# A fused retention and two-layer kernel on one core: the order of operand rounding, product sums and weight rounding in the second layer

## The chip, the cores and the metric

The kernel runs on one NeuronCore of a Trainium2 chip. Its time is the device time of one execution in microseconds (us); less is better. One execution was profiled as well, and all rows of a trace come from that one.

## What is computed

Attention with decays (retention) over 4 batches, 8 heads, 576 positions and 64 values a head gives a matrix x of 2304 x 512. Two layers follow, each of two matrix products with a nonlinearity between them:

```python
ret = (q @ k.T / 8) * Dmat            # per head; Dmat[i, j] = gamma ** (i - j) for i >= j, else 0
x = (ret @ v) as 2304 x 512
h = x @ w_in;  x = maximum(0.01 * h, h) @ w_out          # first layer, 512 -> 2048 -> 512
h = x @ w2_in; y = where(h > 0, h, exp(minimum(h, 0)) - 1) @ w2_out   # second layer
```

All inputs are float32. The kernel keeps float32 accuracy with a faster matmul type (`F32R`): each operand is split in a rounded high part and the low rest, and a product of two numbers takes three matmuls (high x high, high x low, low x high).

## The kernel before, in words

**Tiling.** The 2304 rows are four blocks of 512 and a small one of 256 (`SIZES`). The 2048 middle columns are four quarters `q` of four tiles of 128. Each layer runs quarter by quarter, in it block by block. The results of a quarter stand in PSUM ("y" banks, four) and are added into `yp` in SBUF at the end of each block (`evac`, line 576 on DVE, line 574 on ACT in the first quarter).

**Order.** Everything stands under a manual schedule: each engine runs its instructions in the order of the program text, and an instruction that waits holds all behind it on its engine. Five queues matter: TensorE (PE), VectorE (DVE), ScalarE (ACT), GpSimd (POOL), and SyncE (SP), which issues the DMAs. Generators cut long chains into steps: `go(steps, n)` runs n steps, `spot(n)` runs n steps of the waiting second matrix products (`pending`), `side()` runs one step of a stage. So the text interleaves TensorE's work with that of the other engines.

**First layer.** A loop over 72 units (`units`, line 584; a unit is one tile of one block, in the small block two tiles). A unit does `moe_h` (product 1, then `gh` and `g` on ACT and `gl` on DVE), and `moe_y` of the unit three before (`LAG`). Beside it the weights are split: `split_a` (two ACT passes from the raw weight), `split_b` (four DVE passes, in steps `split_ops`), `split_c` (ACT rounds the high part, POOL or DVE subtracts the low part).

**Second layer.** Its first matrix product is done with seven products of half-size operands in place of eight (`seventh`, numbers 0 to 6; in the trace 12 matmuls of 256 columns each). It needs sums of operands and sums of results:
- operand sums, `stage(blk)`: from the first layer's `yp` it makes differences `t1` to `t4` (`less`, DVE, line 642), rounds seven tiles (`put`: ACT line 636, then POOL or DVE line 638), and sends them to DRAM in four transfers (`send`, line 648). They come back as `xo` (`load_x`, line 680). The stages of blocks 0, 1 and 2 start at units 60, 64 and 68, that of block 3 behind the loop. The tiles `xs` and `xo` and the weight sums `ws` share one pool of eight slots (`xpool`, tag "x").
- weight sums: `sums_a` (four POOL additions, lines 693 to 696), `sums_b` (ACT rounds, line 705; POOL subtracts, line 706).
- result sums, in `seven`: `copy_of` copies a product from PSUM (ACT, line 844: p1, p5, p53), `add_up` adds (DVE, line 839: c11, c12, c22). Product 3 overwrites the bank of p5, so it waits for that copy; products 5 and 6 go on in the bank that c12 and c22 read, so they wait for these sums. c21 stays in the bank.

Each result then goes through `elu`: two ACT passes (lines 738, 740), one DVE pass (742), an ACT rounding (746) and a DVE subtraction (748) into `gg`, from which `second_y` does the second matrix product in four steps of 12 matmuls (6 in the small block, `small_y`).

A block of `seven` thus runs on TensorE: products 0, 1, 2; a step of `second_y` of the block before; products 3, 4; a step; product 5; a step; product 6; a step. In the first block of a later quarter these steps are the small block's, half as long. In the very first block they are the first layer's last three units. Two weights of a coming use are split in each block (`rounds`), and on DVE these passes stand between the sums:

```python
        p53 = copy_of(z)
        seventh(a, q, blk, 4)
        c12 = add_up(a, p53)
        if r[1]:
            go(rest)
```

Of the kernel before, what the change touches and what calls it, by code (L numbers as in the profile page):

```python
# [10 lines left out]
F32 = mybir.dt.float32  # L11
# [80 lines left out]
def retention_moe(  # L92
# [531 lines left out]
    def stage(blk):  # L624
# [6 lines left out]
        def room(k, ops=2):  # L631
            kept[k] = xpool.tile([P, ops, 2, 2, n], F32R, tag="x", name="xs")

        def put(k, i, x):
            hi, lo = kept[k][:, i, 0], kept[k][:, i, 1]
            nc.scalar.activation(hi, x, AF.Copy)  # L636
            by = nc.gpsimd if i == 0 else nc.vector
            by.tensor_tensor(lo, x, hi.bitcast(F32), ALU.subtract)
# [12 lines left out]
        room(0)  # L651
        put(0, 0, b11)
        put(0, 1, b21)
        yield
        send(0)
        t1 = less(b12, b11)
        room(1)
        put(1, 0, t1)
        put(1, 1, b22)
        yield  # L660
        send(1)
        t2 = less(b22, t1)
        t3 = less(b22, b12)
        room(2)
        put(2, 0, t2)
        put(2, 1, t3)
        yield
        send(2)
        t4 = less(b21, t2)
        room(3, 1)  # L670
        put(3, 0, t4)
# [63 lines left out]
    def elu(c, out, cut):  # L735
# [6 lines left out]
        nc.vector.scalar_tensor_tensor(t, t, -1.0, c, ALU.add, ALU.max)  # L742
        t = t.rearrange("p (s n) -> p s n", s=2)
        hi, lo = out[:, 0, :, cut], out[:, 1, :, cut]
        yield
# [47 lines left out]
    def small_h(q, gg):  # L793

        n = SMALL
        for f in range(FQ):
# [18 lines left out]
            if f % 2:  # L815
                g = bpool.tile([P, DM], F32, tag="t", name="g", bufs=3)
# [38 lines left out]
    def seven(q, blk, room, rounds, keep, side):  # L855
# [4 lines left out]
        r = list(rounds) + [None] * (2 - len(rounds))  # L860

# [7 lines left out]
        seventh(a, q, blk, 0, True)  # L869
        if r[0]:  # L870
            split_a(r[0])
        p1 = copy_of(a)
        if r[0]:
            split_b(r[0])
            load_next()
# [6 lines left out]
        p5 = copy_of(z)  # L882
        spot()
        side()
        g1 = room()
        e11 = elu(c11, g1, slice(0, n))
        go(e11, 3)
        if r[0] and not keep and blk:
            split_c(r[0])
        go(e11)  # L890
        seventh(z, q, blk, 3)
        fetch(2)
        if r[1]:
            split_a(r[1])
            rest = split_ops(r[1])
            go(rest, 3)
# [3 lines left out]
        if r[1]:  # L900
            go(rest)
            load_next()
        e12 = elu(c12, g1, slice(n, 2 * n))
        go(e12, 2)
        spot()
        side()
        for key in r[:1] * (blk == 0) + r[1:] * (blk > 0):
            if key and not keep:
                split_c(key)
# [281 lines left out]
```

## Time and profile before

| | us |
|---|---|
| median of 3 runs | 856.83 (856.0 to 857.05) |
| the profiled execution | 856.92 |
| its span on the core | 855.1 |
| TensorE busy | 814.6 (95%) |
| DVE, ACT, POOL busy | 531.3, 443.5, 176.4 |
| mean granted clock of TensorE | 0.978 |

The span is what the trace covers; 1.8 us lie around it. Granted clock 1.00 is 2.4 GHz, 0.50 is 1.2 GHz. TensorE is the busy engine throughout, so the idle stretches ahead of its matmuls, and the stretches at the lower clock, are where time can lie. The page shows the span in 40 slices of 21.4 us, each digit the busy share in tenths:

```profile
PE   9899999999999999998896889989999899989998
...
PEclk9999999999999999999897989999999999999999
```

The second layer's first block begins at 444.30; its quarters follow from 561, 656 and 751.

### The profile page before, as it was taken

The numbers are of one execution on the slowest core, as the hardware profiler recorded it, in microseconds if no ns is written. First come the engines' busy times: TensorE is split into PE (matmuls) and PEld (weight loads), VectorE is DVE, ScalarE is ACT, GpSimd is POOL, SyncE is SP. The second block draws the span as 40 slices with busy tenths as digits, with TensorE's granted clock in tenths as the row PEclk, the third lists the DMA queues.
The fourth block names the chain that finished last, engine by engine and source line by source line (L and its number), as shares of the span: only waits on it lengthen the run. The fifth ranks groups of instructions, "written<-read, shape, count | busy, mean of one in ns | idle before, by whom it ended". The sixth has DMA issues, their size and how long they took to land.

```text
span 855.1 us, 13359 instructions
## 1 busy us (share of the span) xinstructions
PE 814.6 (95%) x5240; PEld 723.1 (85%) x5240; DVE 531.3 (62%) x861; ACT 443.5 (52%) x755; POOL 176.4 (21%) x160
## 2 busy tenths in 40 slices
PE   9899999999999999998896889989999899989998
PEld 6778888888888888887796779779989799879997
DVE  6998943465266625566677756556775677665453
ACT  3456445662244524454545666667665666554442
POOL 2565521000000000015351323221222113210000
PEclk9999999999999999999897989999999999999999
DMA  9995320121011200026488677446570675525612
GB/s 337 330 307 172 132 87 26 50 74 50 1 50 50 74 25 29 22 74 221 172 295 281 235 252 272 189 172 242 203 268 4 258 253 210 191 89 185 242 51 74
DMA packets 34670, 133.64 MB, mean 156 GB/s; under 512 B 4144, under 2 KB 7472, under 8 KB 26928
## 3 DMA queue, kind: packets, MB, share of 16 engines
q1 hardware_dynamic: 34320, 132.66, 43.5%
q8 instruction: 41, 0.67, 0.3%
q14 instruction: 21, 0.17, 0.1%
q10 hardware_dynamic: 288, 0.14, 0.1%
HBM read 113.38 MB, written 19.40 MB: 155 GB/s over the span
## 4 chain that ended last, share of the span: by engine, by line
PE 35%; DVE 7%; ACT 6%; issue 4%; DVEq 0%; ACTq 0%
PE ps_y L406 18%; PE ps_h L406 17%; DVE c L839 2%; ACT gg L746 1%; DVE t L742 1%; ACT t L738 1%; ACT t L740 1%; DVE raw L367 1%; DVE u L372 1%; DVE u L369 1%; DVE yp L576 1%; ACT yp L574 1%; DVE gg L748 1%; ACT xs L636 0%; ACT u L355 0%
## 5 line engine op out<-in xcount | busy, mean ns | idle before, releaser
L406 PE MATMUL ps_y<-woh,gg 128*128 128x512 f32 x580 | 185.5, 382 | 0.2 <-ACT yp L574 0.2
L436 DVE TENSOR_TENSOR gl<-g,gh 128x512 fp32r<-128x512 f32 x64 | 45.7, 714 | 136.6 <-ACT g L430 136.2
L406 PEld LDWEIGHTS ps_y<-woh,gg 128*128 128x128 f32 x580 | 111.1, 192 | 14.8 <-ACT yp L574 0.7
L406 PE MATMUL ps_h<-xo,ws 128*128 128x256 f32 x768 | 102.4, 290 | 21.4 <-DVE c L839 18.4
L406 PEld LDWEIGHTS ps_h<-xo,ws 128*128 128x128 f32 x768 | 98.5, 205 | 26.4 <-DVE c L839 21.5
L429 ACT ACTIVATE gh<-ps_h 128x512 fp32r<-128x512 f32 x64 | 38.2, 597 | 153.6 <-PE ps_h L406 153.5
L406 PE MATMUL ps_y<-gh,woh 128*128 128x512 f32 x288 | 112.1, 389 | 5.8 <-DVE yp L576 5.6
L406 PE MATMUL ps_y<-gl,woh 128*128 128x512 f32 x288 | 110.5, 384 | 0.0
L406 PE MATMUL ps_y<-wol,gg 128*128 128x512 f32 x290 | 110.3, 380 | 0.0
L406 PE MATMUL ps_y<-gh,wol 128*128 128x512 f32 (+1 forms) x288 | 106.7, 371 | 0.7 <-POOL wol L387 0.7
L406 PE MATMUL ps_h<-xh,wih 128*128 128x512 f32 x256 | 97.7, 382 | 1.0 <-ACT wih L385 0.8
L406 PE MATMUL ps_h<-xh,wil 128*128 128x512 f32 x256 | 97.6, 381 | 0.9 <-POOL wil L387 0.9
L387 POOL TENSOR_TENSOR wol<-u,woh 128x512 fp32r<-128x512 f32 x20 | 26.4, 1322 | 333.0 <-ACT woh L385 333.0
L406 PE MATMUL ps_h<-xo,wih 128*128 128x256 f32 x384 | 70.1, 276 | 4.2 <-DVE c L839 4.2
L748 DVE TENSOR_TENSOR gg<-t,gg 128x512 fp32r<-128x512 f32 x64 | 55.0, 862 | 26.2 <-ACT gg L746 25.1
L406 PEld LDWEIGHTS ps_y<-gh,woh 128*128 128x128 f32 x288 | 55.3, 192 | 14.9 <-issue 6.0
L406 PE MATMUL ps_h<-xl,wih 128*128 128x512 f32 x256 | 66.6, 383 | 0.0
L406 PEld LDWEIGHTS ps_h<-xo,wih 128*128 128x128 f32 x384 | 60.9, 192 | 6.6 <-DVE c L839 5.8
L742 DVE SCALAR_TENSOR_TENSOR t<-t,c 128x512 f32<-128x512 f32 x48 | 37.4, 778 | 45.1 <-ACT t L740 45.1
L406 PEld LDWEIGHTS ps_y<-gh,wol 128*128 128x128 f32 x288 | 55.3, 192 | 8.3 <-POOL wol L387 1.1
L406 PEld LDWEIGHTS ps_y<-gl,woh 128*128 128x128 f32 x288 | 55.2, 192 | 7.4
L406 PEld LDWEIGHTS ps_y<-wol,gg 128*128 128x128 f32 x290 | 55.9, 193 | 5.8
(113 smaller groups left out, 1478.8 us busy)
## 6 DMA issues: line engine op xcount, KB each, us to landing
xo<-x SPq DMA_DIRECT2D x48, 1024.0 KB, 6.4
raw<-in_moe_in SPq DMA_DIRECT2D x32, 512.0 KB, 3.8
raw<-in_moe_out SPq DMA_DIRECT2D x32, 512.0 KB, 3.7
x<-xs SPq DMA_DIRECT2D x12, 1024.0 KB, 6.3
ain<-in_att SPq DMA_DIRECT2D x16, 512.0 KB, 6.9
xo<-x SPq DMA_DIRECT2D x16, 512.0 KB, 4.9
ain<-in_att SPq DMA_DIRECT2D x20, 256.0 KB, 7.4
out<-yp SPq DMA_DIRECT2D x17, 256.0 KB, 2.3
```

What stands on the lines that cost most here:

```text
L367: nc.vector.tensor_scalar(high, high, 0x80000000, None, ALU.bitwise_and)
L369: nc.vector.tensor_scalar(u, u, W_LEAST, W_MOST, ALU.max, ALU.min)
L372: nc.vector.scalar_tensor_tensor(x, x, 3, high, ALU.logical_shift_left, ALU.bitwise_or)
L387: engine.tensor_tensor(l, u, h.bitcast(F32), ALU.subtract)
L406: nc.tensor.matmul(out, w, x, **flags)
L429: nc.scalar.activation(gh, h, AF.Prelu, alpha=0.01)
L436: nc.vector.tensor_tensor(gl, g, gh.bitcast(F32), ALU.subtract)
L574: nc.scalar.activation(t, y[e], AF.Copy)
L576: nc.vector.tensor_tensor(t, t, y[e], ALU.add)
L742: nc.vector.scalar_tensor_tensor(t, t, -1.0, c, ALU.add, ALU.max)
L748: nc.vector.tensor_tensor(lo, t, hi.bitcast(F32), ALU.subtract)
L839: nc.vector.tensor_tensor(t, x, y, ALU.add)
```

## The change

Nothing is computed in another way; the same instructions are issued in another order, from partly other buffers.

- `stage` goes in nine steps in place of five: a step rounds on ACT (`high`), the next subtracts (`low`) and takes the differences for the next pair. In the first layer's loop `side()` is called twice a unit, and behind the loop until no stage is left, so that the stages of blocks 0 to 2 end ahead of `seven`. The last block's stage starts one call later (`late`) and takes two of its four tiles from the pool `big`. `seven` calls `side()` four times in place of three.
- `sums_b` of the first weight pair moves to the unit after `sums_a`; that of later pairs moves from the end of block 2 into block 3, behind the rounding of e11.
- In `seven`: p1 is copied ahead of `split_a`; c11 and e11's two ACT passes stand ahead of `split_b`; e11's last subtraction stands behind c12; the second weight's `split_a` stands behind e11's DVE pass, its `split_b` behind c12 (in the first block of a quarter behind c22) with the last pass behind c22; e12's last subtraction stands behind c22.
- `small_h` has a step more, so that `spot` (matmuls and `evac`) stands ahead of its `elu` passes.

```diff
@@ -629,13 +629,15 @@
         kept = {}
 
         def room(k, ops=2):
-            kept[k] = xpool.tile([P, ops, 2, 2, n], F32R, tag="x", name="xs")
-
-        def put(k, i, x):
-            hi, lo = kept[k][:, i, 0], kept[k][:, i, 1]
-            nc.scalar.activation(hi, x, AF.Copy)
+            where = (big, "big") if blk == NMAIN - 1 and k % 2 == 0 else (xpool, "x")
+            kept[k] = where[0].tile([P, ops, 2, 2, n], F32R, tag=where[1], name="xs")
+
+        def high(k, i, x):
+            nc.scalar.activation(kept[k][:, i, 0], x, AF.Copy)
+
+        def low(k, i, x):
             by = nc.gpsimd if i == 0 else nc.vector
-            by.tensor_tensor(lo, x, hi.bitcast(F32), ALU.subtract)
+            by.tensor_tensor(kept[k][:, i, 1], x, kept[k][:, i, 0].bitcast(F32), ALU.subtract)
...
-        room(0)
-        put(0, 0, b11)
-        put(0, 1, b21)
+        def pair(k, *xs):
+            room(k, len(xs))
+            for i, x in enumerate(xs):
+                high(k, i, x)
+            yield
+            for i, x in enumerate(xs):
+                low(k, i, x)
+
+        yield from pair(0, b11, b21)
+        t1 = less(b12, b11)
         yield
         send(0)
-        t1 = less(b12, b11)
-        room(1)
-        put(1, 0, t1)
-        put(1, 1, b22)
+        yield from pair(1, t1, b22)
+        t2 = less(b22, t1)
+        t3 = less(b22, b12)
         yield
         send(1)
-        t2 = less(b22, t1)
-        t3 = less(b22, b12)
-        room(2)
-        put(2, 0, t2)
-        put(2, 1, t3)
+        yield from pair(2, t2, t3)
+        t4 = less(b21, t2)
         yield
         send(2)
-        t4 = less(b21, t2)
-        room(3, 1)
-        put(3, 0, t4)
+        yield from pair(3, t4)
         yield
         send(3)
-    def elu(c, out, cut):
+    def elu(c, g, j, cut):
...
         nc.vector.scalar_tensor_tensor(t, t, -1.0, c, ALU.add, ALU.max)
+        yield
         t = t.rearrange("p (s n) -> p s n", s=2)
-        hi, lo = out[:, 0, :, cut], out[:, 1, :, cut]
-        yield
+        hi, lo = g[j][:, 0, :, cut], g[j][:, 1, :, cut]
         nc.scalar.activation(hi, t, AF.Copy)
         yield
         nc.vector.tensor_tensor(lo, t, hi.bitcast(F32), ALU.subtract)
@@ -813,6 +816,7 @@
             nc.scalar.activation(t, h[:, n:], AF.Copy)
             nc.vector.tensor_tensor(t, t, h[:, :n], ALU.add)
             if f % 2:
+                yield
                 g = bpool.tile([P, DM], F32, tag="t", name="g", bufs=3)
...
-    def seven(q, blk, room, rounds, keep, side):
+    def seven(q, blk, room, rounds, keep, side, begun=None):
...
+        head = blk == 0
+        g = []
...
@@ -867,12 +874,9 @@
         fetch(0)
         a = bank("h", 4)
         seventh(a, q, blk, 0, True)
+        p1 = copy_of(a)
         if r[0]:
             split_a(r[0])
-        p1 = copy_of(a)
-        if r[0]:
-            split_b(r[0])
-            load_next()
         b = bank("h", 4)
         seventh(b, q, blk, 1, True)
         fetch(1)
@@ -880,53 +884,65 @@
         z = bank("h", 4)
         seventh(z, q, blk, 2, True)
         p5 = copy_of(z)
+        e11 = elu(c11, g, 0, slice(0, n))
+        go(e11, 2)
+        if r[0]:
+            split_b(r[0])
+            load_next()
         spot()
         side()
-        g1 = room()
-        e11 = elu(c11, g1, slice(0, n))
-        go(e11, 3)
-        if r[0] and not keep and blk:
-            split_c(r[0])
-        go(e11)
+        g.append(room())
+        go(e11, 1)
+        if r[1]:
+            split_a(r[1])
+        go(e11, 1)
+        if begun:
+            sums_b(begun)
         seventh(z, q, blk, 3)
         fetch(2)
-        if r[1]:
-            split_a(r[1])
-            rest = split_ops(r[1])
-            go(rest, 3)
         p53 = copy_of(z)
         seventh(a, q, blk, 4)
         c12 = add_up(a, p53)
-        if r[1]:
-            go(rest)
-            load_next()
-        e12 = elu(c12, g1, slice(n, 2 * n))
+        go(e11)
+        if r[0] and not keep and not head:
+            split_c(r[0])
+        e12 = elu(c12, g, 0, slice(n, 2 * n))
         go(e12, 2)
+        rest = split_ops(r[1]) if r[1] else iter(())
+        if not head:
+            go(rest, 3)
+            go(e12, 1)
         spot()
         side()
-        for key in r[:1] * (blk == 0) + r[1:] * (blk > 0):
-            if key and not keep:
-                split_c(key)
-        go(e12)
+        if r[0] and head:
+            split_c(r[0])
+        if not head:
+            go(e12, 1)
         seventh(a, q, blk, 5)
         fetch(3)
         c22 = add_up(a, p5)
-        g2 = room()
-        e22 = elu(c22, g2, slice(n, 2 * n))
+        go(e12, 1 + head)
+        e22 = elu(c22, g, 1, slice(n, 2 * n))
         go(e22, 2)
-        spot(2 if blk == 0 and q > 0 else 1)
-        if r[1] and not keep and blk == 0:
+        go(rest)
+        if r[1]:
+            load_next()
+        go(e12)
+        spot(2 if head and q > 0 else 1)
+        if r[1] and not keep:
             split_c(r[1])
         side()
+        g.append(room())
         go(e22, 1)
         seventh(a, q, blk, 6)
-        e21 = elu(a, g2, slice(0, n))
+        e21 = elu(a, g, 1, slice(0, n))
         go(e21, 2)
         go(e22, 1)
         go(e21, 1)
         over.extend((e22, e21))
-        pending.append(second_y(q, blk, (g1, g2)))
+        pending.append(second_y(q, blk, g))
         spot()
+        side()
@@ -1000,6 +1016,16 @@
                 split_a(begun[-1])
 
         stages = deque()
+
+        def side():
+
+            if stages and next(stages[0], end) is end:
+                stages.popleft()
+
+        def late():
+            yield
+            yield from stage(NMAIN - 1)
+
@@ -1022,9 +1048,12 @@
             moe_h(u)
             for key in rounded:
                 split_c(key)
+            if sums and not weights.get(("s", FT)) and n < 66:
+                sums_b(("i", FT))
+                weights["s", FT] = True
             if rounded == [("i", FT + 1)]:
                 sums_a(("i", FT))
-                sums_b(("i", FT))
+            side()
...
@@ -1052,8 +1081,7 @@
                 moe_y(p)
             if n in (60, 64, 68):
                 stages.append(stage((n - 60) // FQ))
-            if stages and next(stages[0], end) is end:
-                stages.popleft()
+            side()
@@ -1082,18 +1110,15 @@
...
-        def side():
-            if stages and next(stages[0], end) is end:
-                stages.popleft()
-
-        side()
-        stages.append(stage(NMAIN - 1))
+        while stages:
+            side()
+        stages.append(late())
         for q in range(NQ):
             for blk in range(NB):
                 if blk < NMAIN:
                     rounds = [splits.pop(0) for _ in range(min(2, len(splits)))]
                     held = rounds if blk == NMAIN - 1 else []
-                    seven(q, blk, room if (q, blk) != (0, 0) else big_room, rounds, bool(held), side)
+                    seven(q, blk, room if (q, blk) != (0, 0) else big_room, rounds, bool(held), side, begun if held else None)
...
@@ -1101,24 +1126,24 @@
                         )
                     if rounds and blk >= 2:
                         sums_a(rounds[0])
-                        if blk == 2:
-                            sums_b(rounds[0])
+                        begun = rounds[0]
                     continue
                 finish()
                 gg = room()
                 parts = small_h(q, gg)
-                next(parts)
-                next(parts)
+                go(parts, 2)
                 spot()
+                go(parts, 1)
                 for key in held:
                     split_c(key)
                 if held:
                     sums_b(held[0])
-                next(parts)
+                go(parts, 1)
                 if q < NQ - 1:
                     spot()
-                next(parts)
+                go(parts, 1)
                 spot(1 if q < NQ - 1 else 2)
+                go(parts)
                 pending.append(small_y(q, gg))
         spot(2)
```

## Rows read from the trace of the kernel before

**Rows 1.** The page's first part: busy time, share, instructions of each engine.
```profile
PE 814.6 (95%) x5240; PEld 723.1 (85%) x5240; DVE 531.3 (62%) x861; ACT 443.5 (52%) x755; POOL 176.4 (21%) x160
```
**Rows 2.** Waits from 396 on; columns: us in total, times, longest.
```profile
PE ps_h L406 <- DVE c L839: 22.6, 12, 4.2
...
PE ps_y L406 <- DVE yp L576: 5.6, 1, 5.6
...
PE ps_h L406 <- ACT cc L844: 2.8, 1, 2.8
```
**Rows 3.** The same view, TensorE alone, from 562 on.
```profile
PE ps_h L406 <- DVE c L839: 10.6, 7, 3.4
```
**Rows 4.** Three stretches: length, busy time by engine (instructions), clock, DMA share, GB/s.
```profile
405.53:412.36 6.83, 3.68 (x9) 2.99 (x10) 5.81 (x7) 3.16 (x6) 4.80 (x3) 0.50 0.19 77
...
448.48:538.66 90.18, 75.64 (x452) 68.67 (x452) 62.02 (x93) 55.32 (x98) 26.08 (x22) 0.91 0.75 266
...
655.95:678.33 22.38, 19.00 (x123) 17.68 (x122) 17.01 (x26) 13.06 (x23) 2.55 (x2) 0.92 0.56 212
```
**Rows 5.** Timeline at 404 to 409: start, duration, instruction, [idle time before it and releaser].
```profile
403.91 1.06 ACT L705 ACTIVATE ws<-sum 128x1024 fp32r<-128x1024 f32 x1 [4.56 <-POOL sum L696]
...
405.39 0.58 ACT L429 ACTIVATE gh<-ps_h 128x512 fp32r<-128x512 f32 x1
...
408.68 0.77 PE L406 MATMUL ps_y<-gh,woh 128*128 128x512 f32 x1 [5.63 <-DVE yp L576]
```
**Rows 6.** Timeline of the second layer's first block, by engine.
```profile
444.18 2.20 DVE L474 TENSOR_TENSOR gh<-hs,gh 128x256 fp32r<-128x256 f32 x1 [1.15 <-ACT gh L473]
...
450.57 1.18 ACT L636 ACTIVATE xs<-t 128x512 fp32r<-128x512 f32 x2 [2.07 <-PE ps_y L406]
...
453.88 4.29 PE L406 MATMUL ps_h<-xo,ws 128*128 128x256 f32 x24 [2.81 <-ACT cc L844]
...
458.99 0.63 ACT L636 ACTIVATE xs<-t 128x512 fp32r<-128x512 f32 x1 [5.16 <-PE ps_h L406]
...
464.97 2.93 PE L406 MATMUL ps_h<-xo,ws 128*128 128x256 f32 x12 [4.17 <-DVE c L839]
```
**Rows 7.** Timeline of the third quarter's first block in the second layer.
```profile
657.75 2.47 DVE L576 TENSOR_TENSOR yp<-yp,ps_y 128x512 f32<-128x512 f32 x4
...
667.06 0.57 ACT L844 ACTIVATE cc<-ps_h 128x512 f32<-128x512 f32 x1
...
668.78 2.93 PE L406 MATMUL ps_h<-xo,ws 128*128 128x256 f32 x12 [3.38 <-DVE c L839]
```
**Rows 8.** Timeline of other blocks: product 5 of a fourth, a second and a fourth block.
```profile
538.66 1.60 PE L406 MATMUL ps_h<-xo,ws 128*128 128x256 f32 x12 [1.11 <-DVE c L839]
...
592.53 0.68 DVE L839 TENSOR_TENSOR c<-ps_h,cc 128x512 f32<-128x512 f32 x1
...
594.43 1.50 PE L406 MATMUL ps_h<-xo,ws 128*128 128x256 f32 x12
...
634.42 1.60 PE L406 MATMUL ps_h<-xo,ws 128*128 128x256 f32 x12 [0.36 <-DVE c L839]
```
**Rows 9.** Timeline: a POOL pass and a DVE pass beside it.
```profile
526.76 2.38 POOL L706 TENSOR_TENSOR ws<-sum,ws 128x1024 fp32r<-128x1024 f32 x1 [3.33 <-ACT ws L705]
...
527.24 2.45 DVE L748 TENSOR_TENSOR gg<-t,gg 128x512 fp32r<-128x512 f32 x1 [0.70 <-ACT gg L746]
```
**Rows 10.** Groups of instructions, 440 to 560: busy us, mean ns of one, idle before.
```profile
L839 DVE TENSOR_TENSOR c<-ps_h,cc 128x512 f32<-128x512 f32 x12 | 8.2, 681 | 0.0
L372 DVE SCALAR_TENSOR_TENSOR u<-u,raw 128x512 uint32<-128x512 uint32 x8 | 6.1, 757 | 0.3
...
L519 DVE TENSOR_TENSOR yp<-yp,ps_y 128x256 f32<-128x256 f32 x4 | 1.7, 418 | 0.4 <-PE ps_y L406 0.4
...
L357 ACT ACTIVATE last<-raw 128x512 uint32<-128x512 uint32 x8 | 6.2, 777 | 0.0
```
**Rows 11.** DMA issues at 440 to 500: count, KB each, median us to landing.
```profile
x<-xs SPq DMA_DIRECT2D x5, 1024.0 KB, 9.2
```

## The prediction

> **What bounds the kernel now.** I read the engine shares first [rows 1]: TensorE is busy for 814.6 of 855.1 us, and no other engine passes 62%, so the end moves only by what TensorE idles (40.5 us) or runs slowly. The list of its waits comes next [rows 2]. Everything ahead of unit 60, in the last quarter of the first layer, stays as it is. Behind it TensorE waits 31.0 us: 22.6 in twelve waits for a sum `c` (line 839), 5.6 in one for `yp` (line 576), 2.8 in one for a copy `cc` (line 844). From 562 us on it is 10.6 in seven waits [rows 3]. Then the clock: over 448.48 to 538.66 the granted clock is 0.91 and TensorE is busy for 75.64 of 90.18 us; over 655.95 to 678.33 it is 0.92; over 405.53 to 412.36 it is 0.50, the lower level, 1.2 GHz [rows 4]. What it did before each fall was wait: 12 matmuls that take 1.50 us elsewhere [rows 8] take 2.93 behind the waits at 464.97 and 668.78 [rows 6, 7]. So each long wait is paid about 1.5 us more. Last, the timeline in front of each wait: what stood ahead of the awaited instruction on its own engine.
>
> **The change part by part.** All is priced against the profiled execution, 856.92 us (span 855.1, 1.8 around it); the median of the runs shown is 856.83, so nothing has to be shifted.
>
> *Weight sums one unit on.* Before, ACT's rounding of the sums (line 705) waits 4.56 us for POOL's four additions and starts at 403.91; the two units' `gh` behind it on ACT start at 405.39, so DVE's `gl` and the four `yp` additions are late and TensorE waits 5.63 us until 408.68 [rows 5]. Afterwards line 705 stands one unit (5.2 us of matmuls) later, behind that unit's `gh` and `g`; POOL has ended by then. Waits and half clock go: 5.63, and 1.8 of the 3.7 busy us at 0.50, which makes **7.4**. POOL's 2.4 us pass then lies beside the next unit, where POOL is free. If POOL were late anyway, ACT would wait again and up to 7.4 would stay.
>
> *The nine steps and the two pools.* A block still takes seven ACT roundings, seven subtractions and four `t` passes; they are issued in smaller portions, and no rounding stands directly ahead of the subtraction that it feeds. Three of the four stages now end before the second layer starts; the third one's last steps are drained together. Before, the third set (ACT at 450.57) and `split_a` of the first weight stand ahead of the copies p1 and p5, which end just ahead of 453.88; TensorE waits 2.81 for them, and then 4.17 until 464.97, because ACT's last `xs` pass waits for DVE until 458.99, with e11 behind it [rows 6]. After: the chain subtract, `t2`, `t3`, round, subtract, `t4`, round comes through on DVE and ACT in one go ahead of p1. From the row at 444.18 (DVE's 2.20 us beside POOL's sums, still there) I get `t3` at 451.0, `t4` at 453.7, its rounding until 454.3, p1 until 454.9, `split_a` (two passes of 0.65 to 0.78 [rows 10]) 1.3, p5 until 456.8. That is worse than 453.88 by 2.9: product 3 then starts after a wait of 5.8, with another fall of the clock (1.45). But nothing of the stage is left behind it: e11 needs 0.6+0.65 on ACT, 2.3 for `split_b` (four passes of 0.41 to 0.76 [rows 10]) and 2.5 for `yp` on DVE, 0.7, 0.65 for its rounding, 0.6 for p53 and 0.7 for c12, which ends at 463.7, about where TensorE arrives (463.9). So one long wait stays where two were. In the rest of that block I find 1.8 of waiting for the PSUM banks that the small block's eight additions free (8 x 0.42 from 469.7 [rows 10]); in the second block 2.1 in three places, the largest 1.5 at c12 behind the stage's DVE passes. Old price of these two blocks: 22.6 - 10.6 + 2.8 [rows 2, 3] less 1.4 in the fourth block, 13.4 idle, and 0.09 x 90.18 [rows 4] less what fell into idle time, 7.8: together 21.2. New price 5.8 + 1.45 + 1.8 + 2.1 = 11.2. **Gain 10.0**. Bounds: with the last `xs` pass waiting for a transfer to land (9.2 us from issue [rows 11], issued about 449.8, so until 459.0, 5 us more) the gain is 5; with no wait at the second block it is 12. I take 10: by 447 TensorE is done with an operand whose slot can serve.
>
> *Sums in front of rounding, first block of the later quarters.* Here only 6 matmuls (1.46 us) instead of 12 cover each sum. Before: `elu` of the small block and the four `yp` additions (657.75) hold DVE, then `split_b`, and c11 comes behind it though its operands lay ready at 658.95; everything is late, p53 is copied at 667.06, c12 follows, and TensorE waits 3.38 until 668.78 [rows 7]. After, from the same start (655.95): the `yp` additions follow their matmuls (until 657.1), p1 until 659.05, c11 659.9, `split_a` 1.45, p5 661.1, e11's two ACT passes until 662.35 (0.63 each, as in [rows 6]), `split_b` on DVE beside them until 662.7, its DVE pass 663.4, the second `split_a` until 663.8, rounding 664.4, p53 665.0, c12 665.7. TensorE arrives at 665.4. Its wait is 0.3, and 0.3 more for the low half of e12 in front of `second_y`. In three quarters 9.4 of the 10.6 us [rows 3] and three half-clock stretches of 1.5 stand here, 13.9 in all; 1.8 stays: **12.1**. Bounds: no wait at all gives 13.9; c12 as late as before gives 0.
>
> *The other blocks.* 12 matmuls (2.75 us) cover each sum; before, c12 was there at 593.21 and TensorE came at 594.43 [rows 8], 1.2 spare. After, only p53 stands behind more on ACT (the rounding of e11) and `split_b` behind c12 instead of ahead; I work out 1.8 spare at c12, 1.1 to 1.9 at c22. So nothing is lost, and the small waits in the fourth blocks (1.11 and 0.5 in the first quarter, 0.36 and 0.28 in each of the next two [rows 8]) go: **2.8**. What is late next is the low half of e12, which now follows c22 and `split_b`; it ends 2 us ahead of its matmuls.
>
> *Weight sums in the fourth block.* POOL's 2.4 us pass moves beside c12 and e11's low half. The row: a DVE pass of 0.69 takes 2.45 beside it [rows 9]. c12 reads PSUM; its mean is 681 ns over 440 to 560 [rows 10], so I charge the low half alone, 1.8 us, hidden behind the spare at c22. If c12 were held too, 3 x 1.7 = 5 would be lost. The Trainium skill, "SBUF — State Buffer", section "Who interferes with whom", says that a VectorE instruction with two SBUF inputs is blocked by a GpSimd instruction that reads SBUF, and one with a single SBUF input isn't. By that rule the low half is held and c12 not, and the sum stands; the trace agrees.
>
> *DMA.* `load_next` moves behind `split_b`, so behind a later fetch on SP. Raw weights are taken three ahead, operands half a block; cost zero. If the transfers at 9.2 us [rows 11] pile up, an operand could be late once: 3.
>
> Sum: 7.4 + 10.0 + 12.1 + 2.8 = 32.3; 856.9 - 32.3 = 824.6, forecast **825**.
>
> **Rivals.** (a) *The work only moves.* The weight passes set behind c12 make c22 or e12's low half late, and half of the 10.0 + 12.1 comes back: 856.9 - 32.3 + 11 = 836. For it: DVE is busy for 17.0 of 22.4 us in the first block of a quarter [rows 4]. Against: the cover there is three groups of matmuls, and `second_y` needs the low half last.
> (b) *The repeated wait is for room, not order*: the `gg` buffer or the bank of z comes free too late in each quarter's first block. Then 12.1 and 2.8 stay and 840 results. Against: the row at 668.78 names the sum, and p53, its operand, was copied only at 667.06, 3 us behind its product [rows 7]. The Trainium skill, "Perfetto Trace Analysis", section "Optimization Strategy", says that the same gap repeating on the engine that should be full can mean too little SBUF or PSUM for the next tile; by that rule this case would be the likely one, and the trace does not bear it out.
> (c) *Slower: p53 queues behind e11's rounding.* On ACT the copy p53 now stands behind a pass that waits for DVE's e11, which stands behind `split_b` and, in the first quarter, the stage. It decides once p53 is late by more than the 1.8 spare in all 16 blocks: at 4.5 us late, 16 x 2.7 = 43 are lost against 32 won, which gives 868. For it: a single DVE pass was seen stretched from 0.69 to 2.45 [rows 9]. Against: POOL has such a pass in few blocks only.
> (d) *Nothing*: the sums' unit slips, the drain costs what the heads win; 857.
>
> **How the numbers follow.** Forecast 0.63 (816 to 832 with the bounds above: 5 for the transfer, 5 for c12, 2 and 1.8 the other way, and some waits that I have not seen), (a) 0.17, (b) 0.07, (c) 0.08, (d) 0.05. The range 815 to 841 holds the forecast, (a) and (b), about 0.85 with their tails cut. Within 0.2% is 1.7 us, about what a measurement of this kernel can tell from no change. Faster by more: 0.63 + 0.17 + 0.07 and a little of (d), 0.88; the same 0.04; slower 0.08.
>
> **What would show it.** No wait for `yp` near 408. One long wait in front of product 3 of the first block, about 5.8 us, and none over 1.6 behind it. In the first blocks of the later quarters waits of 0.3 at line 839 and a granted clock of 1.00. ACT's line 705 without waiting. It would be wrong if waits for `cc` (line 844) appeared in every block (c), or if line 839's waits kept half of their sum (a).

## The result, and the profile after

The changed kernel takes 827.78 us (median of 4, 825.91 to 828.14) against 856.49 for the kernel before (856.0 to 857.05): ratio 0.966, 95% interval 0.9643 to 0.9677. The forecast was 825. The profiled execution took 828.14, against 856.92 in the profile before, so 28.8 of the forecast 32.3 us came. Of all the executions behind the times in this text one, the profiled one of e1, ran at a granted clock of 0.56 and took 1392 us; nothing here is read from it.

The engine shares of the changed kernel, to be read against [rows 1]:

```profile
PE 801.7 (97%) x5240; PEld 713.2 (86%) x5240; DVE 532.5 (64%) x861; ACT 443.1 (54%) x755; POOL 178.6 (22%) x160
```

TensorE idles 24.6 us of 826.3 in place of 40.5, and is busy for 12.9 less with the same 5240 matmuls: that second part is clock (mean granted clock 0.994 in place of 0.978). The other engines run as many instructions as before. TensorE's waits from 396 us on (all but one of 0.2), in the columns of [rows 2]:

```profile
PE ps_h L406 <- ACT cc L848: 6.4, 3, 5.1
PE ps_y L406 <- DVE yp L576: 2.5, 1, 2.5
PE ps_y L406 <- DVE yp L520: 1.8, 1, 1.8
PE ps_y L406 <- ACT t L741: 0.9, 2, 0.4
PE ps_h L406 <- DVE c L843: 0.8, 2, 0.5
```

The sum `c` (now line 843) has fallen from 22.6 us in twelve waits to 0.8 in two. The later quarters [rows 3, 7] have no wait over 0.43 left: in the third quarter's first block product 5 comes without a wait, in 1.50 us where it took 2.93. Line 843 is DVE's sum c12, which product 5 needs.

```profile
645.48 0.69 DVE L843 TENSOR_TENSOR c<-ps_h,cc 128x512 f32<-128x512 f32 x1 [1.64 <-ACT cc L848]
...
646.41 1.50 PE L406 MATMUL ps_h<-xo,ws 128*128 128x256 f32 x12
```

Two larger waits stay, 2.48 at 406 and 5.14 at 453, and with each the clock falls; at 453 it is already low while TensorE waits. A wait of 1.80 (line 520, at 468.50) has no fall. Stretches, as in [rows 4]; the last one encloses the third quarter's first block:

```profile
407.15:410.23 3.08, 3.08 (x8) 2.36 (x8) 2.79 (x4) 2.01 (x5) 3.08 (x3) 0.50 0.72 298
...
448.24:525.86 77.62, 68.83 (x442) 62.56 (x441) 58.73 (x86) 55.67 (x98) 26.16 (x21) 0.96 0.83 314
451.50:458.30 6.80, 4.66 (x22) 4.67 (x23) 5.82 (x10) 4.64 (x9) 1.26 (x1) 0.50 1.00 411
...
634.40:656.00 21.60, 21.17 (x145) 19.56 (x144) 16.94 (x27) 14.66 (x25) 4.14 (x3) 1.00 0.41 157
```

All kernels here run the 5240 matmuls in the same order, so the start of each can be set against that of the same matmul before. The table gives the time won against the kernel before in each stretch, in us (minus is lost), by one trace each; the last column is the median time. The stretches are cut at 383, 419, 460, 513, 568, 662 and 758 us of the kernel before. The first holds the first weight sums, the second the start of product 3 in the second layer's first block, the third the rest of its first two blocks. Over their first 50 us, where no instruction was moved, the traces differ by -1.3 to 0.2 (the changed kernel -0.7); the table leaves that out.

| kernel | sums | to product 3 | first two blocks | rest of quarter 1 | quarter 2 | 3 | 4 | time, us |
|---|---|---|---|---|---|---|---|---|
| changed | 3.3 | -3.2 | 12.1 | 2.1 | 5.2 | 5.6 | 4.4 | 827.8 |
| predicted | 7.4 | 10.0 for these two | | 14.9 for these four | | | | 825 |
| e1b: first sums alone | 7.6 | -1.7 | 3.5 | -0.8 | -0.1 | -0.1 | -0.2 | 849.8 |
| e2: stage alone | -1.8 | -3.1 | 9.2 | -1.2 | 1.0 | -1.4 | -0.3 | 855.4 |
| e3: order alone | -0.1 | 0.0 | 5.0 | 2.0 | 5.2 | 5.6 | 4.4 | 835.0 |
| e11: all but the stage | 7.5 | -0.5 | 4.9 | 2.0 | 5.2 | 5.6 | 4.4 | 828.3 |
| e6: `split_b` ahead of c11 | 3.4 | -2.6 | 11.1 | -0.9 | 0.4 | 2.5 | 2.4 | 841.3 |
| e7: `t` passes early | 7.7 | 2.4 | 10.6 | 2.1 | 5.2 | 5.6 | 4.4 | 819.4 |
| e8: drain behind p5 | 3.2 | 0.1 | 11.1 | 2.0 | 5.2 | 5.6 | 4.4 | 825.4 |
| e9: e7 and e8 | 7.7 | 3.8 | 10.2 | 2.0 | 5.2 | 5.6 | 4.4 | 818.6 |

A cell holds also what the clock did in that one trace: e1b wins 3.5 in the first two blocks, where its instructions are those of before, and there the clock stayed up with a wait of 2.67 where it had fallen with 4.17.

What falls short is the first column. In front of the wait at 406, by start:

```profile
400.62 0.68 DVE L640 TENSOR_TENSOR xs<-t,xs 128x512 fp32r<-128x512 f32 x1
400.84 1.59 POOL L387 TENSOR_TENSOR wil<-u,wih 128x512 fp32r<-128x512 f32 x1 [4.25 <-ACT wih L385]
401.22 1.76 DVE L644 TENSOR_TENSOR t<-yp,t 128x512 f32<-128x512 f32 x1
403.02 0.63 ACT L636 ACTIVATE xs<-t 128x512 fp32r<-128x512 f32 x1 [2.26 <-DVE t L644]
403.55 0.58 ACT L429 ACTIVATE gh<-ps_h 128x512 fp32r<-128x512 f32 x1
404.65 0.83 DVE L436 TENSOR_TENSOR gl<-g,gh 128x512 fp32r<-128x512 f32 x1 [1.67 <-ACT g L430]
405.40 2.47 DVE L576 TENSOR_TENSOR yp<-yp,ps_y 128x512 f32<-128x512 f32 x4
406.10 1.06 ACT L708 ACTIVATE ws<-sum 128x1024 fp32r<-128x1024 f32 x1 [1.48 <-POOL sum L699]
406.23 0.46 PE L406 MATMUL ps_y<-gh,woh 128*128 128x512 f32 x1 [2.48 <-DVE yp L576]
```

The rounding of the sums (line 708) is no longer in the way: it starts behind the awaited `gh`. In its place stands the stage's rounding of t4, the last of the stage's differences (line 636): it waits 2.26 us for a DVE pass that takes 1.76 beside POOL, and `gh` queues behind it, as it queued behind the sums before [rows 5].

### The profile page after: what moved, and what is told of

Its sections match the earlier page's. It is cut to its first block, busy times and chain, and to the rows that moved or that the text cites. A ratio compares the mean times of both kernels' runs of the same rounds, so it can differ in the third digit from the quotient of the medians.

```text
span 826.3 us, 13323 instructions
## 1 busy us (share of the span) xinstructions
PE 801.7 (97%) x5240; PEld 713.2 (86%) x5240; DVE 532.5 (64%) x861; ACT 443.1 (54%) x755; POOL 178.6 (22%) x160
## 5 line engine op out<-in xcount | busy, mean ns | idle before, releaser
L406 PE MATMUL ps_h<-xo,ws 128*128 128x256 f32 x768 | 96.2, 280 | 6.9 <-ACT cc L848 6.4
L406 PEld LDWEIGHTS ps_h<-xo,ws 128*128 128x128 f32 x768 | 93.7, 196 | 10.4 <-ACT cc L848 7.6
L843 DVE TENSOR_TENSOR c<-ps_h,cc 128x512 f32<-128x512 f32 x48 | 33.1, 690 | 62.2 <-PE ps_h L406 51.3
L749 ACT ACTIVATE gg<-t 128x512 fp32r<-128x512 f32 x64 | 39.9, 626 | 41.5 <-DVE t L745 38.8
L576 DVE TENSOR_TENSOR yp<-yp,ps_y 128x512 f32<-128x512 f32 x96 | 59.6, 679 | 2.4 <-PE ps_y L406 2.4
```

The source lines that it names most:

```text
L406: nc.tensor.matmul(out, w, x, **flags)
L576: nc.vector.tensor_tensor(t, t, y[e], ALU.add)
L749: nc.scalar.activation(hi, t, AF.Copy)
L843: nc.vector.tensor_tensor(t, x, y, ALU.add)
```

## The experiments

**The first sums alone (e1).** Before, with this edit only:

```diff
+            if sums and not weights.get(("s", FT)) and n < 66:
+                sums_b(("i", FT))
+                weights["s", FT] = True
             if rounded == [("i", FT + 1)]:
                 sums_a(("i", FT))
-                sums_b(("i", FT))
```

Expected: 

> The kernel before with one edit: POOL's additions of the first weight pair's sums stay where they are, their rounding passes come one unit later. The prediction's term (ACT's rounding at line 705 holds up the units' gh, and with it yp): the wait of 5.63 at 408 and 1.8 of half clock go, so 7.4 less than before, 849.1. Rival from the trace of after, where TensorE still waits 2.48 at 406 behind a t pass that stands beside POOL: in before the stage's steps lie elsewhere, so if the shortfall comes from the nine-step stage, this edit alone must give the full 7.4 and leave no wait for yp near 406. If instead the term itself was mis-sized (POOL's pass disturbs the next unit), a wait of some 2.5 stays here as well and the time is 853 to 854.

Measured: 850.3, ratio 0.9913 (0.9898 to 0.9928). The trace comes from a second run of the same kernel (e1b). Expected: 

> The same kernel as the first sums alone, for a profile at the usual clock: by its times (850.3, 6.9 less) no wait for yp is to be seen near 406, and behind it the trace is that of before, with 2.81 and 4.17 in the first block of the second layer.

Measured: 849.8, ratio 0.9914 (0.9893 to 0.9936). Its waits have no line 576 left (the rest of them are three of at most 0.2), and line 705 comes behind the unit's `gh` of 401.50 (it still waits 2.87 for POOL there, with no wait of TensorE behind it):

```profile
PE ps_h L406 <- DVE c L839: 21.3, 12, 3.6
PE ps_h L406 <- ACT cc L844: 4.2, 3, 3.0
```

```profile
400.96 0.63 ACT L636 ACTIVATE xs<-t 128x512 fp32r<-128x512 f32 x1 [0.57 <-DVE t L642]
401.50 0.58 ACT L429 ACTIVATE gh<-ps_h 128x512 fp32r<-128x512 f32 x1
...
405.44 1.06 ACT L705 ACTIVATE ws<-sum 128x1024 fp32r<-128x1024 f32 x1 [2.87 <-POOL sum L696]
```

At its place the edit wins 7.6, the predicted 7.4. The term was right for the edit by itself; with the whole change only 3.3 comes.

**The stage alone (e2).** Before, with `stage` in nine steps, the two pools, the new `side()` places and the drain; the rest as before.

```diff
-        side()
-        stages.append(stage(NMAIN - 1))
+        while stages:
+            side()
+        stages.append(late())
```

Expected: 

> The kernel before with the stage in nine steps, the two pools, the new places of the side steps and the drain in front of the second layer; the seven products' order, the small block's order and the weight sums are those of before. By the prediction the two blocks behind the first layer lose their 2.81 + 4.17 and get one long wait for it, but some of the 10.0 there belongs to the seven products' order: 4 to 8 less than before, 849 to 853, with the later quarters' waits of 3.4 at line 839 unchanged. Rival (the nine steps are what matters, the seven's order does little): 830 to 840. Other rival (the drain costs what it saves, without the new order behind it): 855 to 859.

Measured: 855.4, ratio 0.9978 (0.9966 to 0.999): not the 849 to 853 that I expected, but the last rival. Two of its waits:

```profile
PE ps_y L406 <- DVE yp L576: 6.9, 1, 6.9
PE ps_h L406 <- ACT cc L847: 5.1, 1, 5.1
```

The wait for `yp` grows from 5.63 to 6.89, the one in front of product 3 from 2.81 to 5.10; together with the clock that costs 4.9, and the first two blocks win 9.2. Most of the waiting was moved forward.

**The order alone (e3).** The changed kernel with the stage, its steps and the first sums of before:

```diff
-            if sums and not weights.get(("s", FT)) and n < 66:
-                sums_b(("i", FT))
-                weights["s", FT] = True
             if rounded == [("i", FT + 1)]:
                 sums_a(("i", FT))
-            side()
+                sums_b(("i", FT))
```

Expected: 

> The changed kernel with the stage of before, its side steps and the first weight pair's sums as before; the order of the seven products, of the small block and of the later sums is the new one. By the prediction the later quarters keep their gain (12.1 + 2.8 predicted, 12.9 + 2.1 found at the matching matmuls of the changed kernel, and about 2.4 in the first quarter's fourth block), so at least 17 less than before: 835 to 841. If the parts add up, this run's gain and that of the stage alone and of the first sums alone make 28.8 together. Rival (the later quarters gain because operands come in time through the two pools): 848 to 853.

Measured: 835.0, ratio 0.9742 (0.9728 to 0.9757): 22 us of the gain (from 857.2 for the kernel before, measured beside it). From the second quarter on it wins the same as the whole change, with buffers as before. The three parts alone add up to 6.9 + 1.8 + 22.2 = 30.9, two more than the 28.7 of all together.

**All but the stage (e11).** The changed kernel with the stage and its steps as in e3, the sums as changed.

```diff
-        yield from pair(0, b11, b21)
-        t1 = less(b12, b11)
+        room(0)
+        put(0, 0, b11)
+        put(0, 1, b21)
...
```

Expected: 

> The changed kernel with the stage and its side steps as before, the first weight pair's sums one unit on. From the runs so far (order alone 835.0, first sums alone 6.9): if the nine steps and two pools are worth nothing in the changed kernel, 828.0, the same as the changed kernel within 1.5. If they are worth something behind the new order (in the second block the changed kernel gains 5 on the order alone by the matching matmuls), 830 to 833. If they cost, 823 to 826. No wait for yp near 406 is expected here, whichever.

Measured: 828.3, ratio 0.9662 (0.9648 to 0.9676), no different from the changed kernel. The nine steps, their places and the two pools are worth nothing in sum: by the table they win 7.2 in the first two blocks, and lose 4.2 at the sums and 2.7 in front of product 3. There is no wait near 406. The old stage takes t4 ahead of any low half: t4 starts 0.23 before POOL's weight pass and takes 0.69; its rounding waits 0.57, not 2.26. In the changed kernel the low half at 400.62 stands first, so t4 starts 0.38 behind that pass and takes 1.76. DVE, POOL and ACT of this kernel:

```profile
399.97 0.69 DVE L642 TENSOR_TENSOR t<-yp,t 128x512 f32<-128x512 f32 x1
```

```profile
400.20 1.60 POOL L387 TENSOR_TENSOR wil<-u,wih 128x512 fp32r<-128x512 f32 x1 [3.68 <-ACT wih L385]
```

```profile
400.69 0.63 ACT L636 ACTIVATE xs<-t 128x512 fp32r<-128x512 f32 x1 [0.57 <-DVE t L642]
401.23 0.58 ACT L429 ACTIVATE gh<-ps_h 128x512 fp32r<-128x512 f32 x1
```

**`split_b` back ahead of c11 (e6).**

```diff
         if r[0]:
             split_a(r[0])
+            split_b(r[0])
+            load_next()
...
         go(e11, 2)
-        if r[0]:
-            split_b(r[0])
-            load_next()
```

Expected: 

> The changed kernel with the low half of the first weight (split_b) and the next load put back between p1 and c11, where before had them: the sum c11 stands behind two DVE passes again. The prediction's mechanism (in the first block of a quarter DVE's rounding of weights holds up c11 and everything behind it): in each of the later three quarters' first blocks c11 and then c12 are later by 1.3 to 1.5, TensorE waits that much more and some half clock with it, and 1 to 3 more in the first quarter's first block: 832 to 838. In blocks with 12 matmuls a sum the spare of 1.2 to 1.8 hides it. Rival (c11 was not what made c12 late; p53 and ACT's order were): within 1 of the changed kernel, 827 to 829.

Measured: 841.3, ratio 0.9808 (0.9794 to 0.9821): 13.5 us lost by moving four DVE passes and the load behind them, nearly half of the change's gain and more than I expected. It is the mechanism that was predicted, and larger. The later quarters' first blocks lose 1.9 to 2.0 each (3.7 in the second quarter, where the clock falls too); I had allowed that. But the fourth blocks of the first three quarters lose as well, 3.0, 1.2 and 1.0, though 12 matmuls cover each sum there, and there I had expected the spare to hide it; the second and third blocks of the later quarters lose nothing. In the first quarter's fourth block POOL is at work too, and two of the four passes are stretched. DVE's queue there, with c11 last; its operands were there at 518.27 (the copy p1 at 517.68, product 1 at 518.27), so it comes 3.5 late:

```profile
518.71 0.69 DVE L367 TENSOR_SCALAR raw<-raw 128x512 uint32<-128x512 uint32 x1 [0.30 <-ACT u L355]
...
519.73 1.27 DVE L372 SCALAR_TENSOR_TENSOR u<-u,raw 128x512 uint32<-128x512 uint32 x1
521.14 0.69 DVE L374 CUSTOM_DVE_ANT_0 u<-u,last 128x1024 uint16<-128x1024 uint16 x1
521.75 0.68 DVE L843 TENSOR_TENSOR c<-ps_h,cc 128x512 f32<-128x512 f32 x1
```

**One pool (e4).**

```diff
-            where = (big, "big") if blk == NMAIN - 1 and k % 2 == 0 else (xpool, "x")
+            where = (xpool, "x")
```

Expected: 

> The changed kernel, but every xs tile of the stage comes from the one pool, as before the change. The prediction held that the last xs pass must not wait for a transfer to land (9.2 from issue) and put 5 on that, in front of the second layer: 833 with that price paid in the drain. Rival (the pools don't matter, since the drain is set by the chain of subtractions and t passes on DVE): within 1.5 of the changed kernel, 826.5 to 829.5, and the wait in front of product 3 stays at 5.1.

Measured: 827.9, ratio 0.966 (0.9647 to 0.9673), and 5.1 in front of product 3 as in the changed kernel: for the time the pools don't matter.

**The small block's order (e5).**

```diff
             if f % 2:
-                yield
...
-                go(parts, 1)
                 for key in held:
```

Expected: 

> The changed kernel with the small block's order as before (its ELU passes not put off, its last steps before the side work rather than behind it). It sits behind every fourth block and in front of the next quarter's first block. By the prediction the first blocks gain from the seven products' order, so only what the fourth blocks gave can go: 2.8 predicted, so at most 831; half of it as likely, 829. Rival (the small block's order is what lets the later quarters' c12 be in time): 835 to 840, with waits over 2 at the sums of the later quarters' first blocks.

Measured: 828.6, ratio 0.9669 (0.9653 to 0.9684). The trace loses 0.7 in the third quarter and 0.8 in the fourth; the times don't tell it from nothing.

**The `t` passes one step earlier (e7).** The changed kernel, and in `stage`:

```diff
-        yield from pair(0, b11, b21)
         t1 = less(b12, b11)
+        yield from pair(0, b11, b21)
         yield
-        send(0)
-        yield from pair(1, t1, b22)
         t2 = less(b22, t1)
         t3 = less(b22, b12)
+        send(0)
+        yield from pair(1, t1, b22)
         yield
+        t4 = less(b21, t2)
         send(1)
         yield from pair(2, t2, t3)
-        t4 = less(b21, t2)
```

Expected: 

> The changed kernel with the stage's differences t1 to t4 issued one step earlier, ahead of the roundings and subtractions of that step. Theory (the term for the first sums fell short because t passes with two inputs in SBUF stand beside POOL's subtraction, 1.77 instead of 0.69, and ACT's H waits 2.26 for t4): the wait of 2.48 at 406 goes, and with it about 1.2 of half clock; the drain's chain is shorter by 0.7 to 1.5: 823 to 825. Rival (DVE has as many passes as before and one of them is late anyway; or POOL's first-sum pass itself holds the unit's passes): 827 to 829 with a wait of 2 or more at 406.

Measured: 819.4, ratio 0.9576 (0.9557 to 0.9595), 8.4 less than the changed kernel and more than I expected. Three of its five executions took 818.7 to 819.4, two 822.1 and 822.3; the trace is one of the three, and what the two did is not shown. The wait at 406 is gone and the sums' column is 7.7; the wait in front of product 3 is 1.74, with no fall of the clock behind it. ACT in front of the two units' `gh`: t4's rounding doesn't wait. DVE's t4 is as slow here, 1.77 beside a POOL pass, but its result is asked for 4 us later:

```profile
398.45 0.61 ACT L636 ACTIVATE xs<-t 128x512 fp32r<-128x512 f32 x1
398.97 0.58 ACT L429 ACTIVATE gh<-ps_h 128x512 fp32r<-128x512 f32 x1
```

```profile
392.69 1.77 DVE L644 TENSOR_TENSOR t<-yp,t 128x512 f32<-128x512 f32 x1
```

```profile
444.91 2.94 PE L406 MATMUL ps_h<-xo,ws 128*128 128x256 f32 x24 [1.74 <-ACT cc L848]
```

**Low halves on DVE (e13).** The changed kernel, no pass of the stage on POOL:

```diff
-            by = nc.gpsimd if i == 0 else nc.vector
-            by.tensor_tensor(kept[k][:, i, 1], x, kept[k][:, i, 0].bitcast(F32), ALU.subtract)
+            nc.vector.tensor_tensor(kept[k][:, i, 1], x, kept[k][:, i, 0].bitcast(F32), ALU.subtract)
```

Expected: 

> The changed kernel with the stage's low halves all on VectorE, so none on POOL: seven DVE passes of about 0.68 more per block, and no POOL pass of the stage beside the t passes. Theory A (the t passes are late because they are held beside POOL, 1.77 instead of 0.69): t4 ahead of the two units' H comes earlier by about 0.4 to 1.1, the wait of 2.48 at 406 shrinks to 1.4 or less: 824 to 827. Theory B (what matters is that t4 and the subtraction stand in front of the units' H at all, one DVE pass replacing the stretch of the other): the wait stays at 2 to 3 and the drain gets a DVE pass longer: 828 to 830.

Measured: 829.0, ratio 0.967 (0.9656 to 0.9685); the wait at 406 grew to 3.46:

```profile
399.82 2.37 DVE L639 TENSOR_TENSOR xs<-t,xs 128x512 fp32r<-128x512 f32 x2
402.11 1.22 DVE L643 TENSOR_TENSOR t<-yp,t 128x512 f32<-128x512 f32 x1
```

(Four passes of a block move to DVE; the seven in the expectation is a slip.) Theory A falls as I wrote it: without the stage's POOL passes t4 is still held, for 1.22, behind two subtractions that take 2.37. What runs beside them here is POOL's weight pass (400.04 to 401.64) and its sums (from 401.61), not a pass of the stage. Theory B has the time, though the wait is longer than its 2 to 3. How the 2.48 of the changed kernel divides between the stretch of t4 and its place in the queue stays open: e7 changes the place and leaves the stretch, and no run takes away the stretch alone.

**The drain later (e8), and both (e9).** e8 leaves the third stage's last steps to a place behind p5:

```diff
-        while stages:
-            side()
+        side()
         stages.append(late())
...
+        if (q, blk) == (0, 0):
+            while len(stages) > 1:
+                side()
         side()
```

Expected: 

> The changed kernel with the third stage's last steps put behind the copy p5 of the first block instead of in front of the second layer. Theory (the 5.14 of waiting in front of product 3 is the drained stage, which ACT and DVE go through ahead of p1 and p5): the wait falls by 2 or more and the half clock behind it with it, but some of it comes back behind p5: 823 to 826. Rival (what stands in front of product 3 is moved in front of product 4 and its sums, one for one): 827 to 830. Slower is possible if it then meets e11: 831.

Measured: 825.4, ratio 0.9631 (0.9618 to 0.9644): the wait in front of product 3 falls from 5.14 to 2.53, and 1.0 comes back behind it.

e9 has the edits of e7 and e8. Expected: 

> Both of the edits that won: the stage's differences one step earlier, and the third stage's last steps behind p5. If they add up: 819.4 - 2.4 = 817.0. Rival (the early differences have already shortened the wait in front of product 3 to 1.74, so there is little left for the other edit, and its steps meet the chain of e11): 818.5 to 821.

Measured: 818.6, ratio 0.9552 (0.9538 to 0.9565). It is the fastest kernel of the study, 9.1 below the changed kernel, but not to be told from e7, as the rival said: it has no wait in front of product 3, which wins 1.4 by the table, and 0.4 of it comes back behind (product 5 waits 1.38 in place of 0.77).

## Why the prediction was right, and where it was off

*Weight sums, 7.4: the term that was mis-sized; it measured 3.3.* I wrote that line 705 afterwards stands behind the unit's `gh`, and that the wait for `yp` goes. The line does (it is 708 now), and the edit alone wins 7.6 (e1b). But I priced it on the queue of before. The stage's nine steps run in the same units and put a low half ahead of t4; t4 then meets POOL's weight pass, and its rounding is late in front of the same `gh` (e11 has no such wait; e7 takes it away). I had looked for what the nine steps do in the second layer only, and put their steps beside the first layer's last units at nothing, without a reason. I also wrote that POOL has ended by the time the sums are rounded; it hasn't (its last addition runs until 406.06, and line 708 waits 1.48 for it), but no wait of TensorE follows from that.

*Nine steps and pools, 10.0 in the first two blocks: 8.9 came (-3.2 + 12.1).* The forecast wait in front of product 3 was 5.8; it was 5.14, with the drained stage ahead of p1 and p5 as described:

```profile
448.97 1.20 DVE L640 TENSOR_TENSOR xs<-t,xs 128x512 fp32r<-128x512 f32 x1 [0.75 <-issue]
450.09 0.68 DVE L644 TENSOR_TENSOR t<-yp,t 128x512 f32<-128x512 f32 x1
450.86 0.63 ACT L636 ACTIVATE xs<-t 128x512 fp32r<-128x512 f32 x1 [1.98 <-DVE t L644]
451.39 0.58 ACT L848 ACTIVATE cc<-ps_h 128x512 f32<-128x512 f32 x1
...
452.97 0.61 ACT L848 ACTIVATE cc<-ps_h 128x512 f32<-128x512 f32 x1
453.64 5.14 PE L406 MATMUL ps_h<-xo,ws 128*128 128x256 f32 x24 [5.14 <-ACT cc L848]
...
461.24 1.50 PE L406 MATMUL ps_h<-xo,ws 128*128 128x256 f32 x12
```

The next long wait [rows 6] is gone, as forecast (no wait at 461.24). The clock cost 2.2 (24 matmuls take 5.14 here and 2.94 in e7), not 1.45; the banks 1.80, as forecast (more than the 1.6 that the signs allowed); the second block 1.64 in three places, forecast 2.1. What was wrong is the owner. I gave the 10.0 to the stage; the order alone wins 5.0 of it (e3), and the stage's share is paid back at the sums and in front of product 3 (e11).

*First blocks of later quarters and the other blocks, 12.1 + 2.8: 17.3.* One wait of 0.43 is left in each later quarter. The first blocks won 12.5 of it, and c11 behind `split_b` is the cause of 7.8 of that, shown by e6; the other moves in these blocks were not run one by one. (Their three waits before are 2.60, 3.38 and 3.31, so 9.3 and not 9.4.) The fourth blocks won 4.8, where 2.8 was forecast: their waits (1.11 and 0.30 in the first quarter; the forecast's 0.5 is a misreading) were worth more than their idle time. Nothing of this is lost to transfers: none of TensorE's waits from 396 us on is for a DMA.

*The sums in the fourth block.* c12 wasn't held and the low half of e11 was, by 1.1 where I had charged 1.8, with no wait of TensorE behind it:

```profile
523.03 2.37 POOL L709 TENSOR_TENSOR ws<-sum,ws 128x1024 fp32r<-128x1024 f32 x1 [5.67 <-ACT ws L708]
```

```profile
523.54 0.69 DVE L843 TENSOR_TENSOR c<-ps_h,cc 128x512 f32<-128x512 f32 x1 [2.84 <-PE ps_h L406]
524.15 1.80 DVE L751 TENSOR_TENSOR gg<-t,gg 128x512 fp32r<-128x512 f32 x1
```

*The rivals.* (a) and (c) left no sign: line 843 keeps 0.8 of 22.6, and copies wait 0.43 once behind the second block. (b), room: the later quarters win the same with buffers as before (e3), so order was the cause; a kernel with one more buffer wasn't run. (d) is true of the stage by itself (e2) and of nothing else.

*The total.* The terms fell short by 4.1 and 1.1, the later blocks gave 2.4 more, and 0.7 went in the first 50 us: 28.8 in place of 32.3. That the time came within 3 us of 825 is in part luck, misses of both signs.

## What to carry to other kernels

A change of several parts is priced on the queues as they will be, not as they were: the weight sums were priced right by themselves (7.6 alone), met another part in one queue, and 4 us went. In an engine that works in order, a pass that only prepares later work belongs where its own input has long been ready: taking differences one step earlier was worth 8 us here (e7), with no instruction added or taken away. Where the same wait returns in every block, look at what stands ahead of the awaited instruction on its own engine, before thinking of buffers.

## What the runs showed of the hardware

A DVE pass that reads PSUM is not slowed by POOL, one with both inputs in SBUF is: in the changed kernel `c` takes 0.69 us in 33 passes with POOL idle and in 15 beside it, `gg<-t,gg` 0.69 in 45 and 1.28 (at most 1.80) in 19. A DVE pass that starts ahead of POOL's is not held: of all passes with both inputs in SBUF, the 18 that start ahead of the POOL pass beside them take at most 0.69, the 54 that start behind one take 0.81 to 2.02. What I had not expected is that passes with one input in SBUF are slowed too: `raw<-raw` (line 367) takes 0.53 in 53 passes and 0.69 in 11 beside POOL, and in e7 once 1.64:

```profile
394.39 1.64 DVE L367 TENSOR_SCALAR raw<-raw 128x512 uint32<-128x512 uint32 x1
```

```profile
393.87 1.72 POOL L640 TENSOR_TENSOR xs<-t,xs 128x512 fp32r<-128x512 f32 x1
```

The Trainium skill, "SBUF — State Buffer", section "Who interferes with whom", has this case beside the one that the prediction quoted: a `tensor_scalar` can enter a mode that takes the pair of ports shared with GpSimd, and can then contend with it. The page frees a pass with one SBUF input only outside such modes, a condition that the prediction left out. The trace agrees in that such passes are held; in which mode they ran it doesn't show. The page also says that the issue order decides who is blocked; the 18 and the 54 passes agree, and so does t4 in e11 and in the changed kernel (0.69 when it starts ahead of POOL's pass, 1.76 behind its start).

What a wait costs in clock can't be read off its length alone. The clock fell to its lower level with waits of 1.93 (e3), 1.99 (e6, 562.25), 2.48 and 5.14 (changed kernel), and stayed at the upper one with 2.29 (e6, 468.40), 2.67 and 3.14 (e1b, 458.77 and 493.06) and 3.23 (e2, 492.51). Product 5 of the first block in e1b and in e3, the longer wait without and the shorter with a fall:

```profile
458.77 1.60 PE L406 MATMUL ps_h<-xo,ws 128*128 128x256 f32 x12 [2.67 <-DVE c L839]
```

```profile
463.49 2.14 PE L406 MATMUL ps_h<-xo,ws 128*128 128x256 f32 x12 [1.93 <-DVE c L840]
```

And with the same wait in front of product 3 (5.14 and 5.13) the 24 matmuls took 5.14 us in the changed kernel and 4.57 in e4, against 2.94 in e7 at the upper level. So the 1.5 that the prediction adds to each long wait holds for the two waits that it was read from, and not for every wait. Why one is followed by a fall and another isn't, no run here shows.
